# Turning k and q by the identity: one product over 128 rows, or two over 64 rows each

## The chip, the cores and the metric

The kernel runs on one core of a Trainium2 chip. The metric is the device time of one execution in microseconds (us); lower is better. Several runs of the kernel are timed, and one execution is recorded by the hardware profiler, which gives the rows that are quoted below.

## The reference, cut to what matters

The first half is a decaying linear attention over 4 batches, 8 heads, 768 positions and 64 channels, in blocks of 64 positions; the second is a mixer with a token part and a channel part.

```python
for b in range(nb):                       # blocks of 64 positions
    intra = einsum('bhic,bhjc->bhij', qb, kb) * Dmask
    intra = einsum('bhij,bhjd->bhid', intra, vb)
    inter = einsum('bhid,bhde->bhie', qb * lam_pow, kv_state)
    out[:, :, sl] = intra + inter
    kv_state = lam_block * kv_state + einsum('bhsd,bhse->bhde', kb * rev_pow, vb)
...
h = relu(x.T @ w_tok1) @ w_tok2
u = x + h.T
return u + relu(u @ w_ch1) @ w_ch2
```

The scores contract over the channels c. q and k arrive from memory with the positions on the partitions, and a product on TensorE contracts over the partitions, so both have to be turned first until the channels lie on the partitions.

## The kernel before

The attention runs over 16 items, each a batch and a pair of heads. For one item the kernel loads k as `kn` and q as `qn`, 128 positions on the partitions. It joins two 64-position blocks to chunks of 128 positions, six chunks a head.

**What is turned, and how.** `turn_k` turns k of every item: 6 products of a 128x128 block with the identity, three into one PSUM bank (h = 0, a bank of the rotating group "sh"), three into another (h = 1, bank "xT"). After each three, ScalarE copies the bank (128x384) to one contiguous half of `kT` (L233). `turn_q_rows` does the same for q (L245, L246), for the first 8 items only (NQ = 8); later items turn q on VectorE (L238). Within a half, the two 64-partition row groups of `kT` and `qT` hold the two 64-position groups or heads that `scores` later contracts apart.

**Who reads the result.** `scores` (L320) multiplies rows 0 to 63 and 64 to 127 of `kT` and `qT` as separate products, alternating between two PSUM banks; its first half (h = 0) reads columns 0 to 383, its second half columns 384 to 767. `scale_q` (L268, GpSimd) reads `qT` too.

**The order around it.** Every engine's queue keeps the order in which the program issues its instructions. Iteration i of the main loop issues on TensorE: `scores(i+1)` (L320), `carry(i)` (L348), `outputs(i, 0)` (L361), `state(i+1)` (the kv products, L281), `outputs(i, 1)` (L361), the turns of item i+2, and then for i of at least 0 two `turn_back` (xp, L386) with the products of the mixer's token part (ph L499, pu L520) placed around them from i = 4 on. On ScalarE the copies of the turns stand behind the copy of `outputs(i, 1)` (L368) and in front of the scaling of k (L262), the conversions of weights (L415, L416, L429) and the casts of `turn_back` (L392). Iterations -2 and -1 have no `turn_back`: there the scores of the item follow its turns at once.

```python
    for i in range(-2, NI):
        if 0 <= i + 1 < NI:
            scores(i + 1)
...
        if i + 2 < NI:
            turn_k(i + 2, 0)
            turn_k(i + 2, 1)
            if i + 2 < NQ:
                turn_q_rows(i + 2, 0)
                turn_q_rows(i + 2, 1)
```

The bank "xT" is used by `carry` for half of its output, by `turn_k` for h = 1 and by `turn_q_rows` for h = 1, one after the other; each must wait until the last reader has copied the bank out.

Of the kernel before, what the change touches and what calls it, by code (L numbers as in the profile page):

```python
# [9 lines left out]
F32 = mybir.dt.float32  # L10
# [15 lines left out]
def kernel(  # L26
# [23 lines left out]
    nc = tc.nc  # L50
    B, H, S, D = q.shape
# [3 lines left out]
    P = 128  # L55
# [36 lines left out]
    def all_of(nm, n):  # L92
        while not all((nm, i) in ready for i in range(n)):
            waiting.popleft()()
# [5 lines left out]
    ident = upool.tile([P, P], F32, name="ident")  # L100
# [10 lines left out]
    def bank(tag, nm, n):  # L111
        nonlocal shared
        if tag == "sh":
            tag = f"sh{shared % 3}"
            shared += 1
        return ps.tile([P, n], F32, tag=tag, bufs=4 if tag == "sc" else 1, name=nm)
# [6 lines left out]
    ap = att.enter_context(tc.tile_pool(name="att", bufs=1))  # L123
# [9 lines left out]
    loaded = {}  # L133
# [67 lines left out]
    def rows_of(x):  # L201
        return slice(x * D, (x + 1) * D)
# [5 lines left out]
    n = 1  # L208
    while n < P:
        nc.vector.tensor_mul(  # L210
            out=lams[:, :, n : 2 * n], in0=lams[:, :, 0:n], in1=lams[:, :, n - 1 : n].broadcast_to([P, 2 * NP, n])
# [3 lines left out]
    for h in range(2):  # L215
        r = rows_of(h)
# [4 lines left out]

    kTs, qTs, qss, kds, weights_of, scored = {}, {}, {}, {}, {}, {}

    def turn_k(i, h):
        kn, _ = loaded[i]
        if h == 0:
            kTs[i] = ap.tile([P, S], F32, tag="kT", bufs=2, name=f"kT{i}")
        kt = bank("xT" if h else "sh", f"kt{i}{h}", 3 * P)
        for m in range(3):
            nc.tensor.transpose(  # L230
                out=kt[:, m * P : (m + 1) * P], in_=kn[:, h, m].rearrange("p x d -> p (x d)"), identity=ident
            )
        nc.scalar.copy(out=kTs[i][:, 3 * h * P : (3 * h + 3) * P], in_=kt)  # L233

    def turn_q(i):
        qTs[i] = ap.tile([P, S], F32, tag="qT", bufs=2, name=f"qT{i}")
        if i >= NQ:
            nc.vector.transpose(out=qTs[i], in_=loaded[i][1])  # L238

    def turn_q_rows(i, h):  # L240
        qt = bank("xT" if h else "sh", f"qt{i}{h}", 3 * P)
        hs = slice(3 * h * P, (3 * h + 3) * P)
        for m in range(3):
            ms = slice((3 * h + m) * P, (3 * h + m + 1) * P)
            nc.tensor.transpose(out=qt[:, m * P : (m + 1) * P], in_=loaded[i][1][:, ms], identity=ident)  # L245
        nc.scalar.copy(out=qTs[i][:, hs], in_=qt)  # L246

    def scale_k(i):
        b, p = pairs[i]
# [14 lines left out]
    def scale_q(i):  # L264
        b, p = pairs[i]
        qss[i] = ap.tile([P, 2, 3, P], F32, tag="qs", bufs=2, name=f"qs{i}")
        for h in range(2):
            nc.gpsimd.tensor_mul(  # L268
                out=qss[i][:, h],
                in0=qTs[i].rearrange("p (h m i) -> p h m i", h=2, i=P)[:, h],  # L270
                in1=lamp[:, p, h, None, :].broadcast_to([P, 3, P]),
            )
# [40 lines left out]
    def scores(i):  # L313
        for h in range(2):
            scored[i, h] = sc = [bank("sc", f"sc{i}{x}{h}", 3 * P) for x in range(2)]
            for m in range(3):
                ms = slice((3 * h + m) * P, (3 * h + m + 1) * P)
                for x in range(2):
                    r = rows_of(x)
                    nc.tensor.matmul(  # L320
                        out=sc[x][:, m * P : (m + 1) * P],
                        lhsT=kTs[i][r, ms],
                        rhs=qTs[i][r, ms],
                        start=True,
                        stop=True,
                    )

    def weigh(i, h):
        b, p = pairs[i]
        for x in range(2):  # L330
            weights_of[i, x, h] = a = ap.tile([P, 3, P], F32, tag="a", bufs=8, name=f"a{i}{x}{h}")
            nc.vector.tensor_mul(  # L332
                out=a,
                in0=scored[i, h][x].rearrange("p (c i) -> p c i", i=P),
                in1=mask[:, 2 * p + h, None, :].broadcast_to([P, 3, P]),
            )
# [274 lines left out]
    def block(k, t):  # L611

        (b, c), (b1, c1) = divmod(2 * k, 3), divmod(2 * k + 1, 3)
        i, j = 3 * (b * NP + t) + c, 3 * (b1 * NP + t) + c1
        return U[:, i : j + 1 : j - i]
# [55 lines left out]
    for i in range(-2, NI):  # L671
        if i == 0:
            nc.vector.memset(scr[:, 3072:], 0)
        if i == NP:
            all_of("w1", 3)
        spare = 30 if i == 6 else 7
        if 0 <= i + 1 < NI:
            scores(i + 1)
            scale_q(i + 1)
            weigh(i + 1, 0)  # L680
        if i >= 0:
            carry(i)
            outputs(i, 0)
        place = state(i + 1) if 0 <= i + 1 < NI else None
        if 0 <= i + 1 < NI:
            weigh(i + 1, 1)
        if i >= 0:
            outputs(i, 1)
        if i + 2 < NI:
            turn_q(i + 2)  # L690
        work = [groups.popleft() for _ in range(take.get(i, 0))]
        if i + 2 < NI:
            if 0 < i + 2 < NP:
                masks(i + 2)
            turn_k(i + 2, 0)
            turn_k(i + 2, 1)
            if i + 2 < NQ:
                turn_q_rows(i + 2, 0)
                turn_q_rows(i + 2, 1)
        if place:  # L700
            place()
        if 1 <= i < NP:
            scale_k(i + 2)
        busy = i >= 8 and len(work) == 5
        if not busy:
            later(*((1 + (i < 6), 1, True) if i >= 4 else (4 if i > 1 else 1, 3)))
        n = early.get(i, len(work) // 4)
        cuts = [0, n, max(n, (3 * len(work) + 1) // 4 if len(work) > 2 else len(work) // 2), len(work)]
        for n in range(3):
            for f in work[cuts[n] : cuts[n + 1]]:  # L710
                f()
                if n == 2 or not busy:
                    later(2 if f in hidden else 1)
            if n < 2 and i >= 0:
                turn_back(i, n)
            if n == 0 and i + 2 < NI and not 1 <= i < NP:
                scale_k(i + 2)
            if n < 2 and i >= 0 and (n == 1 or not busy):
                later(*((1 + (i < 6), 1, n == 1) if i >= 4 else (3, 2) if (i, n) == (3, 1) else (2, 1, True)))
        if 1 <= i < 4:  # L720
            load_w2(i - 1)
        if 0 <= i + 3 < NI and i >= -1:
            load_v(i + 3)
        if -1 <= i < 2:
            load_w1(2 * i + 2, 2 * i + 4)
        if i + 4 < NI:
            load_kq(i + 4)
        if i in loads:
            x = loads.index(i)
            while read < x - 1:  # L730
                later(1)
            load_piece(x // 2, x % 2, words(3)[:, :2048] if x % 2 else scr[:, :2048])
        if 0 <= i < 3:
            convert_w1(i)
        if 2 <= i < 4:
            convert_w2(i - 2)
        if i == 3:
            convert_w2(2)
        if i == 11:
            later(99)  # L740
        if i in turns:
            x = turns.index(i)
            ng, piece = divmod(x, 2)
            a, sg = (words(3) if x % 2 else scr)[:, 2048:3072], scr[:, 3072:]
            waiting.extend(convert_piece(words(3)[:, :2048] if x % 2 else scr[:, :2048], a, sg))
            waiting.append(was_read)
            if ng > 0:
                waiting.append(lambda ng=ng, piece=piece, a=a: park(ng, piece, a))
            elif piece == 0:
                waiting.extend([lambda: None] * 2)  # L750
                waiting.extend(combine(0, lambda: wa, a))
            else:
                waiting.append(lambda a=a: park(0, 1, a))
                waiting.extend([lambda: None] * 2)
                waiting.extend(split_c2(0, lambda: wa, a))
        if i == 13:
            waiting.extend(raw_operand(0, 1, oa, nc.gpsimd, nc.gpsimd))
        if i == 13:
            waiting.extend(raw_operand(0, 2, oa, nc.gpsimd, nc.gpsimd))
# [58 lines left out]
    hs, c_of = {}, {}  # L818
# [524 lines left out]
    for n in range(NQD):  # L1343
        r, g = divmod(n, NG)
        for s in range(7):
# [69 lines left out]
            else:  # L1415
                if n == NG and s == 0:
                    tasks.extend(lambda q_=q_: mm2(NG - 1, 1 - q_ // 4, q_ % 4) for q_ in range(8))
                if n == NG and s == 1:
                    for i in range(4):
                        x = tp.tile([P, 2, CB], F32R, tag="tt", bufs=4, name=f"tt{i}")  # L1420
                        tiles.extend((x[:, 0], x[:, 1]))
                if n == NG + 1 and s == 1:
# [7 lines left out]
                    for t in ("c2h", "c2l"):  # L1430
                        x = w2b.tile([P, JG, DM], F32R, tag=t, name=f"{t}x")
# [31 lines left out]
        if n == NG - 1:  # L1463
# [8 lines left out]
            for t in ("c2h", "c2l"):  # L1472
                x = wa.tile([P, JG, DM], F32R, tag=t, name=f"{t}x")
# [45 lines left out]
```

## Time and profile before

| what | value |
|---|---|
| median of 3 runs | 554.84 us (554.48 to 555.19) |
| span of the profiled execution, first to last instruction | 552.4 us |
| left of the median outside that span | 2.4 us |
| TensorE busy | 537.1 us, 97% of the span |
| TensorE weight loads busy | 455.1 us, 82% |
| VectorE busy | 386.8 us, 70% |
| ScalarE busy | 250.2 us, 45% |
| GpSimd busy | 275.9 us, 50% |

For the profiled execution the span is what is recorded; the runs that were timed give the total beside it. Busy time of TensorE counts a product from its start to its modelled end. Products are pipelined, so neighbouring ones overlap in these records, and the distance from one start to the next is what a product costs in a stream.

### The profile page before, as it was taken

Reading aid. Unit: us, or ns where it says so; the run is one execution under the profiler, and the core shown is the slowest. Engines: PE = TensorE matmul, PEld = TensorE weight load, DVE = VectorE, ACT = ScalarE, POOL = GpSimd, SP = SyncE. Lnnn points to the kernel's source line nnn. Section 1 sums busy time; section 2 is a strip of 40 time slices with the busy share of each in tenths; the row PEclk is TensorE's granted clock in tenths of the full one; section 3 lists DMA queues with packets and bytes.
Section 4 is the critical chain, followed back from the end, with each engine's and each line's share of the span. In section 5 each row is a group of like instructions: output and inputs, shape, how many; then the busy total and the mean of one; then the engine's idle time right before and its main releaser. Section 6 shows DMA issues by size and latency. Waiting matters only on the chain.

```text
span 552.4 us, 9745 instructions
## 1 busy us (share of the span) xinstructions
PE 537.1 (97%) x3710; PEld 455.1 (82%) x3710; DVE 386.8 (70%) x588; ACT 250.2 (45%) x463; POOL 275.9 (50%) x264
## 2 busy tenths in 40 slices
PE   6999999999999999999999999999998999999996
PEld 5888989999999988788888888888886888888885
DVE  4667776677865868688995657498578864474464
ACT  3477544654534456455554344344464343233111
POOL 5555636552442777556769635545878123141000
PEclk9999999999999999999999999999999999999999
DMA  9999878698500497956777899677346987554007
GB/s 188 245 264 220 189 143 222 143 201 199 133 1 6 172 296 253 361 190 250 285 284 268 179 239 304 206 246 273 133 125 211 205 197 294 225 169 156 0 2 151
DMA packets 162942, 108.12 MB, mean 196 GB/s; under 512 B 132560, under 2 KB 147408, under 8 KB 162896
## 3 DMA queue, kind: packets, MB, share of 16 engines
q1 hardware_dynamic: 153168, 86.92, 58.4%
q10 hardware_dynamic: 9728, 20.58, 10.0%
q8 instruction: 29, 0.48, 0.4%
q14 instruction: 17, 0.14, 0.1%
HBM read 75.50 MB, written 31.98 MB: 195 GB/s over the span
## 4 chain that ended last, share of the span: by engine, by line
PE 81%; DVE 6%; ACT 5%; DMA 4%; POOL 2%; issue 2%; SPq 1%; DVEq 0%; ACTq 0%
PE b L858 15%; PE gb L1114 9%; PE po L1059 9%; PE d L858 7%; PE gc L1114 7%; PE ph L499 6%; PE pu L520 5%; PE sc L320 4%; PE xT L361 4%; PE a L858 4%; DMA raw<-in_moe_w_ch_dram 3%; PE xT L348 2%; PE gb L1059 2%; PE gc L1059 2%; PE kv L281 2%
## 5 line engine op out<-in xcount | busy, mean ns | idle before, releaser
L302 POOL COPY st<-sv 64x192 f32<-64x192 f32 (+1 forms) x32 | 15.7, 492 | 58.8 <-DVE sv L289 57.9
L1072 DVE TENSOR_TENSOR uT<-po,uT 128x512 f32<-128x512 f32 x48 | 32.8, 684 | 10.2 <-PE po L1059 9.6
L1059 PE MATMUL po<-hh,c2l 128*128 128x512 f32 x96 | 37.8, 394 | 0.0
L1059 PE MATMUL po<-hl,c2h 128*128 128x512 f32 x96 | 37.7, 392 | 0.0
L1059 PE MATMUL po<-hh,c2h 128*128 128x512 f32 x96 | 37.6, 392 | 0.0
L368 ACT COPY uT<-xT 128x384 f32<-128x384 f32 x32 | 15.2, 479 | 47.2 <-PE xT L361 47.2
L332 DVE TENSOR_TENSOR a<-sc,mask 128x384 f32<-128x384 f32 x64 | 32.1, 543 | 2.4 <-PE sc L320 2.3
L268 POOL TENSOR_TENSOR qs<-qT,lamp 128x384 f32<-128x384 f32 x32 | 32.6, 1040 | 0.0
L879 POOL TENSOR_TENSOR hl1x<-t,hh1x 128x512 fp32r<-128x512 f32 x8 | 10.6, 1326 | 41.8 <-ACT hh1x L873 41.8
L1129 DVE TENSOR_TENSOR uT<-gb,uT 128x512 f32<-128x512 f32 x40 | 26.1, 683 | 3.8 <-PE gb L1114 3.8
L393 DVE TENSOR_TENSOR xlo<-xp,xhi 128x384 fp32r<-128x384 f32 x32 | 17.7, 552 | 15.7 <-ACT xhi L392 15.2
L499 PE MATMUL ph<-xhi,w1h 128*128 128x256 f32 x96 | 28.3, 295 | 0.3 <-DVE hl L504 0.3
L499 PE MATMUL ph<-xhi,w1l 128*128 128x256 f32 x96 | 27.2, 283 | 0.0
L499 PE MATMUL ph<-xlo,w1h 128*128 128x256 f32 x96 | 27.1, 283 | 0.0
L361 PE MATMUL xT<-a,vn 128*64 128x128 f32 x384 | 27.1, 277 | 0.0
L320 PE MATMUL sc<-qT,kT 64*128 64x128 f32 x384 | 27.1, 290 | 0.0
L320 PEld LDWEIGHTS sc<-qT,kT 64*128 64x128 f32 x384 | 23.9, 197 | 3.0 <-issue 1.2
L858 PE MATMUL b<-o,c1h 128*128 128x512 f32 x72 | 25.2, 391 | 0.0
L858 PE MATMUL a<-o,c1h 128*128 128x512 f32 x72 | 25.2, 391 | 0.0
L879 POOL TENSOR_TENSOR tt<-t,tt 128x512 fp32r<-128x512 f32 x12 | 17.0, 1420 | 14.6 <-ACT tt L873 14.6
L520 PE MATMUL pu<-w2h,hh 128*128 128x384 f32 x64 | 23.2, 363 | 0.9 <-DVE uT L525 0.5
L289 DVE TENSOR_TENSOR_SCAN sv<-keep,kv 128x320 f32<-128x320 f32 x16 | 13.1, 816 | 13.3 <-PE kv L281 6.6
(417 smaller groups left out, 1737.6 us busy)
## 6 DMA issues: line engine op xcount, KB each, us to landing
c1h<-k SPq DMA_DIRECT2D x12, 896.0 KB, 5.5
c1l<-k SPq DMA_DIRECT2D x12, 896.0 KB, 7.6
raw<-in_moe_w_ch_dram SPq DMA_DIRECT2D x7, 1024.0 KB, 5.7
vn<-in_v_dram SPq DMA_DIRECT2D x16, 384.0 KB, 6.1
k<-c1h ACTq DMA_DIRECT2D x6, 896.0 KB, 5.2
k<-c1l ACTq DMA_DIRECT2D x6, 896.0 KB, 4.1
out_dram<-y SPq DMA_DIRECT2D x72, 64.0 KB, 2.5
c2lx<-k SPq DMA_DIRECT2D x7, 512.0 KB, 4.2
```

Of the source, the lines that this page charges most:

```text
L268: nc.gpsimd.tensor_mul(out=qss[i][:, h], in0=qTs[i].rearrange("p (h m i) -> p h m i", h=2, i=P)[:, h], in1=lamp[:, p, h, None, :].broadcas ...
L320: nc.tensor.matmul(out=sc[x][:, m * P : (m + 1) * P], lhsT=kTs[i][r, ms], rhs=qTs[i][r, ms], start=True, stop=True,)
L332: nc.vector.tensor_mul(out=a, in0=scored[i, h][x].rearrange("p (c i) -> p c i", i=P), in1=mask[:, 2 * p + h, None, :].broadcast_to([P, 3, P]),
L361: nc.tensor.matmul(out=xT[h * D : (h + 1) * D, m * P : (m + 1) * P], lhsT=vns[i][:, h, c, :], rhs=weights_of[i, x, h][:, m, :], start=Fals ...
L499: nc.tensor.matmul(out=ph, lhsT=w[:, c, fs], rhs=x[:, c], start=(i == 0), stop=(i == 3 * NC - 1))
L520: nc.tensor.matmul(out=pu, lhsT=h[:, kk, cs], rhs=w[:, kk, ss], start=(i == 0), stop=(i == 3 * NK - 1))
L858: nc.tensor.matmul(out=c[into], lhsT=w[:, WI[o], ct], rhs=x[:, ct], start=(first and i == 0), stop=(i == 5), skip_group_check=True,)
L879: nc.gpsimd.tensor_sub(out=B_[key][1], in0=src, in1=B_[key][0].bitcast(F32))
L1059: nc.tensor.matmul(out=po, lhsT=w[:, jj, cs], rhs=h, start=(i == 0), stop=(i == 3 * JG - 1), skip_group_check=n >= NG)
L1072: nc.vector.tensor_add(out=ub, in0=two(po), in1=ub)
L1114: nc.tensor.matmul(out=G[into, t], lhsT=w2[:, v, j, t * P : (t + 1) * P], rhs=x, start=(o in (5, 1, 2) and not second and i == 0), stop=(i ...
L1129: nc.vector.tensor_add(out=ub, in0=two(G[into, t]), in1=ub)
```

## The change

Each block of 128 rows is turned by two products of 64 rows: rows 0 to 63 with the upper left 64x64 of the identity into the "sh" bank, rows 64 to 127 with the lower right 64x64 into the "xT" bank. The six blocks of an item are issued in turn, the two halves of a block one after the other, and all twelve products come before the two copies. Each bank now holds one 64-row half of all six blocks, and each copy writes every other run of 64 columns of `kT` or `qT`.

```diff
-    def turn_k(i, h):
+    def turn(i, to, block, nm):
+        banks = [bank("xT" if y else "sh", f"{nm}{i}{y}", 3 * P) for y in range(2)]
+        for n in range(6):
+            for y in range(2):
+                r = rows_of(y)
+                nc.tensor.transpose(out=banks[y][:, n * D : (n + 1) * D], in_=block(n)[r], identity=ident[r, r])
+        view = to.rearrange("p (n y s) -> p n y s", y=2, s=D)
+        for y in range(2):
+            nc.scalar.copy(out=view[:, :, y], in_=banks[y].rearrange("p (n s) -> p n s", s=D))
+
+    def turn_k(i):
         kn, _ = loaded[i]
-        if h == 0:
-            kTs[i] = ap.tile([P, S], F32, tag="kT", bufs=2, name=f"kT{i}")
-        kt = bank("xT" if h else "sh", f"kt{i}{h}", 3 * P)
-        for m in range(3):
-            nc.tensor.transpose(
-                out=kt[:, m * P : (m + 1) * P], in_=kn[:, h, m].rearrange("p x d -> p (x d)"), identity=ident
-            )
-        nc.scalar.copy(out=kTs[i][:, 3 * h * P : (3 * h + 3) * P], in_=kt)
+        kTs[i] = ap.tile([P, S], F32, tag="kT", bufs=2, name=f"kT{i}")
+        turn(i, kTs[i], lambda n: kn[:, n // 3, n % 3].rearrange("p x d -> p (x d)"), "kt")
...
-    def turn_q_rows(i, h):
-        qt = bank("xT" if h else "sh", f"qt{i}{h}", 3 * P)
-        hs = slice(3 * h * P, (3 * h + 3) * P)
-        for m in range(3):
-            ms = slice((3 * h + m) * P, (3 * h + m + 1) * P)
-            nc.tensor.transpose(out=qt[:, m * P : (m + 1) * P], in_=loaded[i][1][:, ms], identity=ident)
-        nc.scalar.copy(out=qTs[i][:, hs], in_=qt)
+    def turn_q_rows(i):
+        turn(i, qTs[i], lambda n: loaded[i][1][:, n * P : (n + 1) * P], "qt")
...
-            turn_k(i + 2, 0)
-            turn_k(i + 2, 1)
+            turn_k(i + 2)
             if i + 2 < NQ:
-                turn_q_rows(i + 2, 0)
-                turn_q_rows(i + 2, 1)
+                turn_q_rows(i + 2)
```

## Rows read from the trace of the kernel before

**Rows 1.** The page: engines, busy us, share of the span, instructions; then the chain by engine
```profile
PE 537.1 (97%) x3710; PEld 455.1 (82%) x3710; DVE 386.8 (70%) x588; ACT 250.2 (45%) x463; POOL 275.9 (50%) x264
...
PE 81%; DVE 6%; ACT 5%; DMA 4%; POOL 2%; issue 2%; SPq 1%; DVEq 0%; ACTq 0%
```

**Rows 2.** The chain that ended last, first items: start us, us, what
```profile
7.01 0.88 PE qt L245 x3
7.88 2.86 PE sc L320 x24
...
13.22 0.55 PE qt L245 x3
```

**Rows 3.** The same chain from 18.2 us, iteration 0
```profile
18.30 0.49 ACT uT L368
...
18.82 0.87 ACT kT L233 x2
```

**Rows 4.** Tile kt: duration ns min/median/max, first and last start, forms
```profile
L230 PEld LDWEIGHTS kt<-ident,kn x96: 137/140/232, 4.3 to 150.0; 128*128 128x128 f32 x96
L230 PE MATMUL kt<-ident,kn x96: 272/273/477, 4.3 to 150.1; 128*128 128x128 f32 x96
L233 ACT COPY kT<-kt x32: 478/484/500, 5.2 to 150.4; 128x384 f32<-128x384 f32 x32
```

**Rows 5.** Tile sc, products of 64 rows
```profile
L320 PEld LDWEIGHTS sc<-qT,kT x384: 182/188/336, 7.8 to 157.5; 64*128 64x128 f32 x192
L320 PE MATMUL sc<-qT,kT x384: 271/272/577, 7.8 to 157.6; 64*128 64x128 f32 x192
```

**Rows 6.** Tile kv, products with 64 moving columns
```profile
L281 PE MATMUL kv<-vn,kd x320: 218/222/367, 10.7 to 159.9; 128*64 128x64 f32 x160
```

**Rows 7.** TensorE in order of time, iteration 0: start us, us, what, [idle before]
```profile
18.18 0.87 PE L230 MATMUL kt<-ident,kn 128*128 128x128 f32 x6
18.89 0.49 PE L245 MATMUL qt<-ident,qn 128*128 128x128 f32 x3
19.74 0.55 PE L245 MATMUL qt<-ident,qn 128*128 128x128 f32 x3 [0.36 <-ACT kT L233]
20.12 0.82 PE L386 MATMUL xp<-ident,uT 128*128 128x128 f32 x6
20.87 1.61 PE L320 MATMUL sc<-qT,kT 64*128 64x128 f32 x24
...
24.01 0.75 PE L281 MATMUL kv<-vn,kd 128*64 128x64 f32 x20
```

**Rows 8.** ScalarE in order of time, iteration 0
```profile
18.82 0.86 ACT L233 COPY kT<-kt 128x384 f32<-128x384 f32 x2
19.57 0.50 ACT L246 COPY qT<-qt 128x384 f32<-128x384 f32 x1
20.32 0.48 ACT L246 COPY qT<-qt 128x384 f32<-128x384 f32 x1 [0.25 <-PE qt L245]
```

**Rows 9.** TensorE in order of time, iteration -1
```profile
11.73 0.87 PE L230 MATMUL kt<-ident,kn 128*128 128x128 f32 x6
...
13.70 1.61 PE L320 MATMUL sc<-qT,kT 64*128 64x128 f32 x24
```

**Rows 10.** TensorE in order of time, iteration -2
```profile
4.31 1.71 PE L230 MATMUL kt<-ident,kn 128*128 128x128 f32 x6 [4.31 <-DMA kn<-in_k_dram]
```

**Rows 11.** TensorE in order of time, iteration 7, an item without q turns
```profile
83.81 0.88 PE L230 MATMUL kt<-ident,kn 128*128 128x128 f32 x6
84.46 0.44 PE L520 MATMUL pu<-w2h,hh 128*128 128x384 f32 x1
84.74 0.34 PE L520 MATMUL pu<-w2h,hl 128*128 128x384 f32 x1
84.92 0.34 PE L520 MATMUL pu<-w2l,hh 128*128 128x384 f32 x1
```

**Rows 12.** The chain in iteration 3
```profile
42.14 0.56 ACT kd L262
```

## The prediction

> **What bounds the kernel now.** I read the page's busy shares first, then the chain of waits by engine: TensorE is busy for 97% of the span and carries 81% of the chain [rows 1]. A busy TensorE is not yet a TensorE that does useful work all the time, so next I followed the chain in order of time through the attention, where all the turns lie. In the first iterations it does not stay on TensorE. In iteration 0 it goes from the copy of the outputs to the two copies of kT, all on ScalarE [rows 3], and back to TensorE with the second three turns of q. The reader should see there that TensorE stands idle for 0.36 us until ScalarE has copied kT [rows 7]: the "xT" bank has one copy, and q's second half needs it. The third thing to read is TensorE and ScalarE in order of time, to see which work runs beside which [rows 7, 8]: q's first three turns run while ScalarE still copies kT, and the first copy of qT is out before the second three turns are done. The fourth is the later items without turns of q [rows 11], where the next products follow the turns without a wait.
>
> **What a whole turn costs.** In the stream of six xp turns the step from start to start is (0.82 - 0.273) / 5 = 0.109 us [rows 4, 7]. The six of kt take 0.87 us, 0.05 more than xp, which is the first step after a change of the array's form (the products before them have 64 columns).
>
> **What a half turn costs.** No row shows a turn over 64 rows; two other products bracket it. The score products use row halves with 128 moving columns and come every (1.61 - 0.272) / 23 = 0.058 us [rows 5, 7], about half of 0.109: the two row halves do work side by side. The kv products have 64 moving columns and come every (0.75 - 0.222) / 19 = 0.028 us, so two in 0.056 [rows 6, 7]. A pair of half turns has both: row halves, and 64 moving columns. The lower end for a pair is half of a whole turn, 0.054 us; the upper end is a pair of score products, 0.116 us, where the 64x128 weight load and not the moving columns sets the step. The weight loads tell which is nearer: a score load of 64x128 takes 188 ns, that of a whole turn 140 ns with twice the rows [rows 4, 5]. Turns are thus loaded faster than ordinary products, for a reason that lies in the turn and not in its rows. I take 0.058 us a pair.
>
> The Trainium skill, in "TensorE: Matmul & The Clock Gate", section "LDWEIGHTS (loading the stationary operand)", says that a load costs its columns divided by 1.2, whatever its rows. By that rule each half would load for an estimated 107 ns, more than its 64 columns take to move, and splitting would save nothing per block; the 140 ns of a turn against the 188 ns of a score load speak against using one figure for both, and by the rule the sum is that of the second rival below.
>
> **A change of form.** The qt products end at 19.74 + 0.55 = 20.29 and xp, of the same form, starts at 20.12, 0.17 before that end. The xp end at 20.94 and the score products, of 64 rows, start at 20.87, only 0.07 before [rows 7]. So a change of form costs 0.10, and another 0.05 in the first step. The new turns add one such change to every item: from 64 rows back to 128.
>
> **Twelve half turns.** First to last pair 5 x 0.058 + 0.05 = 0.34 us; with the 0.22 that a product of 64 columns lasts [rows 6] they end 0.56 after they start, where six whole turns took 0.87. The next product of another form comes at 0.56 - 0.07 = 0.49, with the slower first step 0.54; before it came at 0.87 - 0.17 = 0.70. A turn saves 0.16, half of what its shorter products promise. For pu the same comes out: its second product stood 0.93 after the first kt (84.74 - 83.81), with a first step of 0.28 against 0.18 [rows 11], and will stand at 0.49 + 0.28 = 0.77.
>
> **Items 8 to 15, only k.** Eight turns at 0.16: -1.3 us. Their copies are not on the way of the next products. This holds where TensorE sets the pace; where VectorE does, it is less, so 0 to 1.3.
>
> **Items 2 to 4.** kt starts at 18.18 and ends at 18.74. ScalarE copies the outputs until 18.79 [rows 3] and starts on kT at 18.82 as before; shorter turns gain nothing there. Both copies are done at 19.68, and q's turns, which now all need "xT" from their second product on, start at 19.74. Before, only three were left at this point, and half of q was about to be copied [rows 8]. Now twelve halves run to 20.30, and both copies come after: 20.33 to 21.19, with 0.86 for the two as for kT [rows 8]. The scores read both interleaved halves at once, so they start 0.06 later at 21.25, where they started at 20.87 [rows 7]. The xp products lie between (20.23 to 21.10) and no longer cover the copies. +0.38 us in each of three items: +1.1. Behind the late copies stand the scaling of k and the casts on ScalarE, and scale_q on GpSimd; they move by the same 0.4 and are taken in by it.
>
> **Item 1.** No xp stands between turn and scores, and before, the scores began on the half that was there. kt runs 11.73 to 12.29, copies 12.32 to 13.18, q's turns 13.24 (13.22 before [rows 2]) to 13.80, copies 13.83 to 14.69, scores 14.75 against 13.70 [rows 9]: +1.05.
>
> **Item 0.** Here all runs at about half the pace (1.71 us for six turns [rows 10]). q's second half begins at 7.01 and its three turns take 0.88 [rows 2]; as pairs, at twice 0.058, some 0.3 less, to 7.57. Then two copies to 8.46 and the scores at 8.52, against 7.88 in the chain: about +0.7 with the 0.07 by which products start ahead of their piece in the chain.
>
> **Items 5 to 7.** In iteration 3 the chain runs through ScalarE: k's scaling stands behind qT's second copy [rows 12] and moves by the same 0.38; 0 if that copy is not what holds it. Items 6 and 7 are followed by products that don't need qT; there only the turns count: after the wait, xp or ph came 0.55 - 0.17 = 0.38 later, now 0.54. +0.16 each, 0.3 in all.
>
> **Sum.** 0.7 + 1.05 + 1.1 + 0.4 + 0.3 - 1.3 = +2.3 us. On the profiled execution's 552.4 us span that is 554.7; 2.4 us lie outside the span in the median of 554.84, so 557.1. The copies cost nothing new of themselves: 384 columns each as before, their runs cut to 64.
>
> **Rivals.** *The early loss is taken up (not slower).* Items 0 to 7 lose 3.6 us. If a later step of the attention is held by something that doesn't move with them, such as a transfer of weights or a conversion that VectorE and ScalarE have to finish anyway, the 3.6 vanish there and the 1.3 of the later items stay: 553.5. It decides from 1.3 us taken up upward (about 555.8 at that point). For it speaks that the chain leaves TensorE for 19% of the span [rows 1]; against it, that these steps stand in program order behind the copies that move, and that the DMA share of the chain is 4%. Chance 0.1.
>
> *The split saves nothing.* A pair takes 0.116, because the halves load at the score products' pace or don't overlap as turns. Then twelve halves end after 0.85, as six whole ones did, and the changed order of copies is all that is left: scores at 21.78 (+0.91) in items 2 to 5, +1.6 in item 1, about +1.0 in item 0, 0.7 in items 6 and 7, and in items 8 to 15 +0.13 each for the change of form: 3.6 + 1.6 + 1.0 + 1.4 + 1.0 = +8.7, 563.5. The page's rule above leads here. For it: only the 48 ns between two weight loads argue for a shorter load. Chance 0.2.
>
> *Halves one after the other, each at 0.111.* Some 0.58 more in each of 24 turns on top of that: about 577. The score products speak against it. Chance 0.03.
>
> The forecast has the remaining 0.67. Its own range is 556.4 (no loss in items 5 to 7) to 558.5, with 559 if the slow pace at the start lasts through item 1's scores, which took 2.86 us in the chain at that pace and 1.61 after it [rows 2, 9]. The range for 8 in 10 takes in the second rival and leaves out the first where it is complete: 554.6 to 564.2. A difference under 0.2%, 1.1 us, can't be told from no change here. Faster needs the first rival nearly whole: 0.06; within 0.2%, the rest of it and a small forecast: 0.11; slower 0.83.
>
> **What the profile after would show.** Pairs of half turns 0.058 apart, six in 0.56 with their end; kT's copies in iteration 0 where they were, relative to the copy of the outputs; no turn of q before them; TensorE idle for about 0.9 us instead of 0.36 there; the scores waiting for qT in items 1 to 4; in the later items the next product 0.16 sooner after kt. The forecast is wrong if the pairs are 0.11 apart, if the scores don't wait for both copies of qT, or if the shift at 62 us (about +3.6) is gone before 160 us by more than the 1.3 that the later items give back.

## The result, and the profile after

The changed kernel takes 560.72 us in the median of 4 runs (559.59 to 561.91), the kernel before 554.66: a ratio of 1.011, 95% interval 1.0098 to 1.0123. The way was forecast, the size was not: +6.1 us where +2.3 stood, though inside the range (554.6 to 564.2). The profiled execution took 560.19 us with a span of 558.4.

The page, which answers to [rows 1]: TensorE has 144 products more and is busy for 1.2 us less, in a span 6.0 us longer.

```profile
PE 535.9 (96%) x3854; PEld 453.1 (81%) x3854; DVE 388.0 (69%) x588; ACT 250.1 (45%) x463; POOL 275.7 (49%) x264
```

The tile kt, as in [rows 4]: duration min/median/max, first and last start, forms.

```profile
L229 PEld LDWEIGHTS kt<-ident,kn x192: 134/140/226, 4.8 to 156.3; 64*128 64x128 f32 x192
L229 PE MATMUL kt<-ident,kn x192: 221/223/367, 4.8 to 156.4; 64*128 64x64 f32 x192
L232 ACT COPY kT<-kt x32: 479/484/489, 6.2 to 157.0; 128x384 f32<-128x384 f32 x32
```

The weight load of a half turn is recorded with the 140 ns of a whole one, and a product lasts 223 ns, as the kv products with 64 columns did (222) [rows 6]. The copies cost what they cost before (484 ns), although they write runs of 64.

TensorE in order of time, from item 0's first turn to iteration 0 (compare [rows 10], [rows 9] and [rows 7]): start, us, what, idle time before and what ended it.

```profile
4.79 0.58 PE L229 MATMUL kt<-ident,kn 64*128 64x64 f32 x6 [4.79 <-DMA kn<-in_k_dram]
...
7.13 0.90 PE L229 MATMUL qt<-ident,qn 64*128 64x64 f32 x11 [0.27 <-ACT kT L232]
8.90 2.93 PE L319 MATMUL sc<-qT,kT 64*128 64x128 f32 x24 [0.88 <-ACT qT L232]
...
13.03 0.90 PE L229 MATMUL kt<-ident,kn 64*128 64x64 f32 x12
...
14.88 0.58 PE L229 MATMUL qt<-ident,qn 64*128 64x64 f32 x11 [0.89 <-ACT kT L232]
16.36 2.19 PE L319 MATMUL sc<-qT,kT 64*128 64x128 f32 x24 [0.90 <-ACT qT L232]
...
22.31 0.59 PE L229 MATMUL kt<-ident,kn 64*128 64x64 f32 x12
22.96 0.27 PE L229 MATMUL qt<-ident,qn 64*128 64x64 f32 x1
23.90 0.58 PE L229 MATMUL qt<-ident,qn 64*128 64x64 f32 x11 [0.67 <-ACT kT L232]
24.42 0.87 PE L385 MATMUL xp<-ident,uT 128*128 128x128 f32 x6
25.46 1.61 PE L319 MATMUL sc<-qT,kT 64*128 64x128 f32 x24 [0.17 <-ACT qT L232]
```

In iteration 0 the twelve halves of k end 0.59 us after their start (0.56 was forecast, 0.87 stood before). One half of q follows, into the free bank; the second needs the other bank, and eleven halves wait until k has been copied out. Then the scores wait for both copies of q: they start 3.15 us after the first turn of k, where it was 20.87 - 18.18 = 2.69 [rows 7].

ScalarE in the same iteration (compare [rows 8]):

```profile
22.43 0.48 ACT L367 COPY uT<-xT 128x384 f32<-128x384 f32 x1 [0.76 <-PE xT L360]
22.99 0.86 ACT L232 COPY kT<-kt 128x384 f32<-128x384 f32 x2
24.55 0.86 ACT L232 COPY qT<-qt 128x384 f32<-128x384 f32 x2 [0.70 <-PE qt L229]
```

Before, the first copy of q stood at 19.57, joined to k's two. Now ScalarE stands idle for 0.70 us until q's halves are done.

Where the 6.0 us of span arose, by the first start of kt in an item (from TensorE in order of time):

| stretch | before, us | after, us | forecast | measured |
|---|---|---|---|---|
| start to item 0's turn | 4.31 | 4.79 | 0 | +0.48 |
| turn of item 0 to turn of item 2 | 13.87 | 17.52 | +1.75 | +3.65 |
| item 2 to item 6 | 29.17 | 30.99 | +1.5 | +1.82 |
| item 6 to item 8 | 23.30 | 23.81 | +0.3 | +0.51 |
| item 8 to item 15 | 78.83 | 78.88 | -1.1 | +0.05 |
| item 15 to the end | 402.90 | 402.41 | -0.2 | -0.49 |

The loss in items 2 to 7 is near the forecast. The first row is the landing of the first k, before any turn; in the other runs it came 0.05 to 0.52 us later than in the trace before, also where items 0 and 1 were turned as before, so it is not put down to the change. Two entries are far from the forecast: the first two items lost 1.9 us more, and the later items gave nothing back. The first is seen in the stage's windows: us, then busy time of TensorE, weight loads, VectorE, ScalarE and GpSimd (with the number of instructions), then the granted clock, the DMA share and GB/s. Three windows of the kernel after, and one of the kernel before:

```profile
11.00:14.00 3.00, 2.98 (x41) 2.50 (x39) 1.39 (x4) 0.04 (x1) 1.19 (x2) 1.00 1.34 218
14.00:18.00 4.00, 2.22 (x33) 2.09 (x35) 3.34 (x8) 1.69 (x4) 3.26 (x6) 0.90 1.31 220
18.00:19.50 1.50, 1.50 (x24) 1.28 (x24) 0.35 (x1) 0.00 (x0) 0.99 (x2) 0.50 1.14 287
```

```profile
14.00:18.00 4.00, 4.00 (x88) 3.76 (x85) 2.54 (x6) 0.77 (x2) 3.32 (x4) 1.00 1.30 213
```

From 14 to 18 us TensorE is busy for 2.22 of 4.00 us, waiting twice for 0.9; then its granted clock is 0.50, the lower level of 1.2 GHz, while it ends the scores of item 1 and starts on the outputs of item 0. In the kernel before it is busy all through 14 to 18 us, and the clock shows 1.00 in every one of these windows. The 1.00 of the first window is no measure of the pace: twelve halves take 0.90 us at 13.03 us and 0.59 later, so TensorE is still slow there, where the kernel before had six turns in 0.87 us at 11.73 us [rows 9].

The second entry is seen in the later items. The waits of TensorE's weight loads (PEld) for ScalarE's copy of the outputs (uT) from 70 to 170 us: who waited for whom, us in total, times, longest.

```profile
PEld pu L519 <- ACT uT L367: 0.8, 4, 0.2
PEld xp L385 <- ACT uT L367: 0.4, 2, 0.2
PEld ph L498 <- ACT uT L367: 0.4, 2, 0.2
```

Eight items, eight waits of 0.2 us, none of which stood in the trace before. The product after k's turn takes the shared bank from which ScalarE copies half of the outputs (L367). That copy ends about 0.6 us after the first turn of k, whichever way k is turned, and the next product starts 0.65 us after that turn in both kernels (before, 0.71 in two of the eight items). Before, the six whole turns lasted as long as the copy; ScalarE in the kernel before, in the iteration of [rows 11]:

```profile
83.93 0.48 ACT L368 COPY uT<-xT 128x384 f32<-128x384 f32 x1 [0.76 <-PE xT L361]
```

### The profile page after: what moved, and what is told of

The parts are those of the page before. It is cut to its first block, busy times and chain, and to the rows that moved or that the text cites. A ratio compares the mean times of both kernels' runs of the same rounds, so it can differ in the third digit from the quotient of the medians.

```text
span 558.4 us, 10027 instructions
## 1 busy us (share of the span) xinstructions
PE 535.9 (96%) x3854; PEld 453.1 (81%) x3854; DVE 388.0 (69%) x588; ACT 250.1 (45%) x463; POOL 275.7 (49%) x264
## 4 chain that ended last, share of the span: by engine, by line
PE 65%; DVE 5%; DMA 4%; ACT 2%; issue 1%; DVEq 0%; ACTq 0%
PE b L855 15%; PE gb L1111 9%; PE po L1056 8%; PE d L855 7%; PE gc L1111 7%; DMA raw<-in_moe_w_ch_dram 4%; PE pu L519 4%; PE a L855 4%; PE ph L498 3%; PE gb L1056 2%; PE gc L1056 2%; PE xT L360 1%; PE sc L319 1%; PE xT L347 1%; PE xp L385 1%
## 5 line engine op out<-in xcount | busy, mean ns | idle before, releaser
L367 ACT COPY uT<-xT 128x384 f32<-128x384 f32 x32 | 15.3, 480 | 49.2 <-PE xT L360 49.2
L319 PE MATMUL sc<-qT,kT 64*128 64x128 f32 x384 | 27.6, 294 | 2.3 <-ACT qT L232 2.1
L319 PEld LDWEIGHTS sc<-qT,kT 64*128 64x128 f32 x384 | 24.4, 199 | 5.3 <-ACT qT L232 3.5
```

Source lines behind the costliest of these rows:

```text
L319: nc.tensor.matmul(out=sc[x][:, m * P : (m + 1) * P], lhsT=kTs[i][r, ms], rhs=qTs[i][r, ms], start=True, stop=True,)
```

## The experiments

Each ratio is to the kernel before, timed beside it on the same chip. Two theories stood after the result. The first: the order of turns and copies costs some 0.46 us in each early item, the clock 1.6 to 1.9 us at the start, and a bank takes the later items' gain. The second: 64-row products cost time themselves, in every item alike.

**Which items lose.** `whole_for_two` turns items 0 and 1 as before, and the rest by halves; `halves_for_two` is its counterpart.

```diff
-            turn_k(i + 2)
+            if i + 2 >= 2:        # whole_for_two;  i + 2 < 2 in halves_for_two
+                turn_k(i + 2)
+            else:
+                whole_k(i + 2, 0)
+                whole_k(i + 2, 1)
...                                # q in the same way
```

> Items 0 and 1 are turned as before (whole products, a copy after each three), items 2 to 15 by halves. The theory: of the 6.0 us of span that the change costs, 3.7 us arise before item 2's turn starts, because the scores of items 0 and 1 follow the turns directly and because TensorE's clock then rises about 2.4 us later and falls back once (granted 0.50 in 18.0 to 19.5 us). With whole turns there the 3.7 us are gone: +2.3 us over the kernel before, about 557.0. The rival, that every item with turns of q loses the same: two of eight such items are spared, a quarter of 6, so +4.5 us, about 559.2.

Measured: 557.75 us, ratio 1.0051 (1.0038 to 1.0065). The start took 13.63 us from turn to turn against 13.87 before, so its loss is gone. Items 2 to 5 lost 0.43 to 0.46 each. What the theory did not have is one more fall of the clock: item 6 lost 1.76 us, where it loses 0.30 in the changed kernel. TensorE was busy for 2.48 of the 4.00 us from 48 to 52, where the kernel before has 3.78:

```profile
48.00:52.00 4.00, 2.48 (x44) 1.97 (x40) 3.97 (x9) 2.62 (x6) 2.52 (x3) 0.92 1.29 245
52.00:54.00 2.00, 2.00 (x12) 1.88 (x10) 1.97 (x3) 1.45 (x3) 1.88 (x3) 0.50 1.12 203
```

> Only items 0 and 1 are turned by halves, k and q; items 2 to 15 as before. The counterpart of whole_for_two, which left +3.0 us without them. The theory, that these two items carry the copies' delay (1.7 us as forecast) and most of the late clock: +3 to +3.7 us, about 558, and the clock falls back before 21 us as in the changed kernel; nothing is lost or gained after item 2. The rival, equal loss per item: +1.5 us, about 556.2.

Measured: 557.53 us beside 553.82, ratio 1.0066 (1.0052 to 1.0079). The start took 16.57 us, +2.7, and no item after it lost anything (the shift is 3.03 us at item 2 and 2.97 at item 15). The recorded execution took 556.54 us, 1.0 us under the median. The clock fell here too (granted 0.51 in this window):

```profile
15.00:18.50 3.50, 3.11 (x28) 2.89 (x32) 2.03 (x4) 0.34 (x1) 3.31 (x4) 0.51 1.25 218
```

Equal loss per item is refuted by both: items 0 and 1 alone cost 3.0 us in the trace and 3.7 in the median, items 2 to 15 alone 3.0 in the median, about 1.5 of it by the fall of the clock in item 6.

**The clock.** `after_filled` gives TensorE products to do in its waits; their results are overwritten.

```diff
+        for n in range((8 if i < 2 else 10) if nm == "qt" else 0):
+            r = rows_of(0)
+            nc.tensor.transpose(out=banks[0][:, n % 6 * D : (n % 6 + 1) * D], in_=block(n % 6)[r], identity=ident[r, r])
...
+            for _ in range(4 if i < 2 and h == 0 else 0):
+                nc.tensor.transpose(out=sc[0][:, :P], in_=ident, identity=ident)
```

> The changed kernel with extra products whose results are overwritten, put where TensorE stands idle: before q's twelve halves the upper halves once more (10 products of 64 rows, 0.56 us, in a wait of 0.67 to 0.89 us), and ahead of the scores of items 0 and 1 four turns of the identity (0.85 us at the slow pace, in a wait of 0.88 and 0.90 us). The theory, that 1.9 of the 6.0 us are TensorE's clock, which rises later and falls back (0.50 in 18.0 to 19.5 us) because TensorE does less at the start: the clock rises near 11.4 us as before and stays, and the time falls by 1.5 to 2 us to about 558.9, though TensorE does more. The rival, that the late start comes from waits alone: no gain, 560.7 or slower.

Measured: 559.22 us, ratio 1.0086 (1.0073 to 1.0099). With more work the kernel is 1.5 us faster. The start took 15.90 us in place of 17.52, and the clock stayed up:

```profile
14.00:18.00 4.00, 3.30 (x55) 2.74 (x57) 3.65 (x8) 1.41 (x4) 3.22 (x5) 1.00 1.31 220
18.00:21.00 3.00, 3.00 (x74) 2.71 (x66) 0.99 (x3) 0.81 (x2) 1.03 (x2) 1.00 0.67 201
```

TensorE in order of time at the start of `after_filled` (its four turns of the identity, L319, write to sc):

```profile
4.66 0.58 PE L232 MATMUL kt<-ident,kn 64*128 64x64 f32 x6 [4.66 <-DMA kn<-in_k_dram]
...
9.67 2.73 PE L324 MATMUL sc<-qT,kT 64*128 64x128 f32 x24
12.33 0.80 PE L283 MATMUL kv<-vn,kd 128*64 128x64 f32 x20
13.07 0.59 PE L232 MATMUL kt<-ident,kn 64*128 64x64 f32 x12
...
16.09 1.61 PE L324 MATMUL sc<-qT,kT 64*128 64x128 f32 x24 [0.31 <-ACT qT L235]
...
20.56 0.59 PE L232 MATMUL kt<-ident,kn 64*128 64x64 f32 x12
```

The scores of item 0 stand here in the kernel before:

```profile
7.81 2.94 PE L320 MATMUL sc<-qT,kT 64*128 64x128 f32 x24
```

| stretch of the start, us | before | after | `after_filled` |
|---|---|---|---|
| item 0's first turn to its scores | 3.50 | 4.11 | 5.01 |
| those scores to item 1's first turn | 3.92 | 4.13 | 3.40 |
| item 1's first turn to its scores | 1.97 | 3.33 | 3.02 |
| those scores to item 2's first turn | 4.48 | 5.95 | 4.47 |

With the clock up, item 1 loses 1.05 us between its turns and its scores, and nothing behind them. The 1.6 us that come back are a net figure: the added products hold item 0's scores back by 0.9 us. By stretches the changed kernel's 3.65 us are some 2.0 of the clock (0.21 and 1.47 behind the scores, and 1.36 - 1.05 = 0.31 in item 1's turns) and some 1.7 of the copies (0.61 + 1.05), an estimate from these three traces; the forecast had 1.75 for the copies. `before_warm` asks whether the clock at the start is worth something to the kernel before.

```diff
+    warm = bank("sc", "warm", P)
+    for _ in range(13):
+        nc.tensor.transpose(out=warm, in_=ident, identity=ident)
```

> The kernel before with 13 turns of the identity, written to a bank that nothing reads, between the end of the identity's making (1.4 us) and the landing of the first k (4.3 us), where TensorE stands idle. The theory of the clock: with work from 1.4 us on, the half pace of the first items ends some 3 us sooner than at 11.4 us, and half of that is gained: 553.2 (-1.5 us). The rival, that the pace of the start is bound to something other than TensorE's own work: 554.7, no difference.

Measured: 553.92 us, ratio 0.9988 (0.9980 to 0.9997). The full pace is there earlier, the scores of item 0 take 1.61 us and not 2.94, but little is gained. TensorE in order of time (the view begins at 3 us, with the last seven of the thirteen), and the piece of the chain that ends before item 1's q:

```profile
2.72 1.70 PE L189 MATMUL warm<-ident 128*128 128x128 f32 x7
...
7.60 1.61 PE L323 MATMUL sc<-qT,kT 64*128 64x128 f32 x24
```

```profile
6.09 6.29 DMA qn<-in_q_dram
```

Item 1's q lands at 12.38 us, and that sets the start then. The theory was right on the pace and wrong on its worth: in the kernel before, the slow first items lie in front of that transfer, and q's turns of item 1 begin at 12.44 us there and at 12.43 here. In the changed kernel the slow pace reaches past it, to the turns at 13.03 us. This is the one version faster than both, by 0.7 us (0.2 to 1.1).

**The later items.** `halves_from_eight` splits only k of items 8 to 15; `k8_other_bank` adds one line after it, `shared += 1`, by which the next product takes the following shared bank.

> Only k of items 8 to 15 is turned by halves; all else is as before. The prediction on record gave these eight turns -1.3 us (0.16 each), about 553.4. The theory after the result: the product that follows takes the shared bank that held half of the outputs, and it waits for ScalarE's copy of them, which ends as late as before; so no difference, 0 to +0.2 us, about 554.8.

Measured: 554.7 us, ratio 0.9998 (0.9989 to 1.0007): no difference, and eight waits of 0.2 us for the copy of the outputs as in the changed kernel.

> As halves_from_eight, but after k's twelve halves one shared bank is passed over, so that the next product goes to the bank of the kv products, which VectorE has read by then, and not to the one that ScalarE still copies out. The theory, that this bank is what takes the gain away: the next product starts about 0.13 to 0.15 us sooner in up to eight items, -0.8 to -1.1 us, about 553.8. The rival, that the change of the array's form takes the gain: as halves_from_eight, 554.7.

Measured: 557.07 us, ratio 1.0048 (1.0036 to 1.0060). TensorE in iteration 8, in `halves_from_eight` and then in `k8_other_bank`:

```profile
95.97 0.59 PE L229 MATMUL kt<-ident,kn 64*128 64x64 f32 x12
96.61 0.39 PE L517 MATMUL ph<-xhi,w1h 128*128 128x256 f32 x1
```

```profile
95.09 0.59 PE L229 MATMUL kt<-ident,kn 64*128 64x64 f32 x12
95.61 0.39 PE L517 MATMUL ph<-xhi,w1h 128*128 128x256 f32 x1
```

The next product comes 0.52 us after the turn's start in place of 0.64. From item 9's turn to item 10's and from there to item 11's the time is 0.13 and 0.12 us shorter than before, about what was forecast for a turn (0.16). Item 8's next product came as early, but a later wait for VectorE took the gain. In iteration 9 the wait that takes the first one's place shows: the bank of the kv products is still being read by VectorE.

```profile
108.08 0.39 PE L517 MATMUL ph<-xhi,w1h 128*128 128x256 f32 x1 [1.70 <-DVE sv L307]
```

After that wait the clock falls once more (granted 0.60 from 108 to 112 us), and this one item is 2.9 us longer. The three intervals that follow are 0.13 to 0.21 us longer each: item 12 waits for VectorE again, and in items 13 and 14 a later product takes the bank of k's own turns and waits 0.3 us for ScalarE to copy them out.

```profile
PEld ph L517 <- ACT kT L232: 0.7, 2, 0.3
```

So the bank is shown to be what held the next product back, and the next bank in the round is worse for the kernel.

**Order against halves.** `whole_alternating` has the changed order with whole products.

```diff
         for n in range(6):
-            for y in range(2):
-                r = rows_of(y)
-                nc.tensor.transpose(out=banks[y][:, n * D : (n + 1) * D], in_=block(n)[r], identity=ident[r, r])
+            nc.tensor.transpose(out=banks[n % 2][:, n // 2 * P : (n // 2 + 1) * P], in_=block(n), identity=ident)
...
```

> Whole 128-row products in all items, but with the changed order: block by block into the two banks in turn, both copies after the last product, each copy taking every other block of 128 columns. The theory, that the loss comes from copies and turns that wait for each other and not from 64-row products: slower than the changed kernel, since six whole turns end 0.87 us after their start and not 0.56, twice per item with q; items 2 to 5 at about +0.95 each, items 0 and 1 at +3 to +5 with the late clock, items 6 and 7 at +0.5 each: 562 to 564. The rival, that half-row products or their change of the array's form are what costs: near the kernel before, 554.5 to 555.5.

Measured: 560.26 us, ratio 1.0097 (1.0083 to 1.0110), between the two and much nearer to the theory: the order alone costs what the change costs. Items 2 to 5 lost 0.54 to 0.77 us each, more than with halves (0.44 to 0.46) and less than expected; items 2 to 7 together lost 3.46 us, with halves 2.33. At the start 2.4 us were lost and not 3 to 5, with halves 3.65: TensorE was busier, 2.81 of the 4.00 us from 14 to 18, and the clock stayed at 1.00.

```profile
14.00:18.00 4.00, 2.81 (x39) 2.30 (x42) 3.09 (x7) 1.61 (x4) 3.42 (x6) 1.00 1.31 212
```

What halves save in items 2 to 7, whole turns save at the start.

`q_halves_from_two` and `k_halves_from_two` take the two tensors apart; items 0 and 1 are as before.

> Only q of items 2 to 7 is turned by halves; k and items 0 and 1 as before. The theory, that q's twelve halves all wait for k's copies and both copies of q come after them: the whole loss of whole_for_two, +0.46 us in items 2 to 5, +0.3 and +0.2 in items 6 and 7, +2.3 us, about 557; more, up to 558.6, if TensorE's clock falls back once as it did there. The rival, that k's and q's halves share the loss: half of it, 555.8.

Measured: 556.1 us beside 553.82, ratio 1.0038 (1.0026 to 1.0051). Items 2 to 5 lost 0.40 to 0.41 us each, nearly the 0.46 of the theory; item 6 lost nothing and item 7 0.17, where 0.3 and 0.2 stood. Without k's halves the clock did not fall.

> Only k of items 2 to 15 is turned by halves; items 0 and 1 and all of q as before. The theory, that ScalarE's copy of the outputs and not the turn of k sets the start of k's copies, and that q's order is what costs: no difference, 554.6, with iterations 0 to 2 at 7.16 us each as before. The rival, that the halves of k cost by their later first copy or their change of form: +0.3 to +0.46 in each of items 2 to 5, 556 or more.

Measured: 557.13 us beside 553.82, ratio 1.0058 (1.0045 to 1.0071), against the theory and far above it. Yet the attention is not where it is lost: items 2 to 5 took 0.04 us more each, and the last turn of k comes at the same time after the first. One transfer of weights near 216 us took 10.01 us (8.14 before), and the span ended 6.15 us after the start of the last product (5.11 before). `k_halves_again` is the same kernel on another chip.

> The kernel of k_halves_from_two once more, on whatever chip it gets. There the attention part took as long as before (last turn of k 0.1 us off), and 2.5 us were lost after it, in one transfer of weights of 10.01 us where 8.14 stood before and in the tail after the last product. If that belongs to the kernel, the time is again 3 us over the kernel before; if it belongs to that run's chip or placement, 554.5 to 555 beside a kernel before at 554.7, which is what the theory said of k's halves (no difference).

Measured: 557.53 us beside 554.49, ratio 1.0061 (1.0045 to 1.0077), with 10.22 us for the same transfer and 6.06 at the end:

```profile
216.34 10.22 DMA raw<-in_moe_w_ch_dram
```

It belongs to this kernel then, and not to the chip, and lies in transfers 60 us behind the turns. Why it does is open. `q_past_the_bank`, below, has some of it (9.08 us for the transfer, and 0.85 us more after item 15's turn); in the other runs that transfer takes 7.9 to 8.5 us. The changed kernel does not have it (its part after item 15's turn is 0.5 us shorter than before), so it is no part of the 6 us.

**The bank in q's way.** `q_past_the_bank` is the changed kernel with q's second bank from the shared group; `q_past_whole` the kernel before with the same.

```diff
-        banks = [bank("xT" if y else "sh", f"{nm}{i}{y}", 3 * P) for y in range(2)]
+        banks = [bank("xT" if y and nm == "kt" else "sh", f"{nm}{i}{y}", 3 * P) for y in range(2)]
```

> The changed kernel with one edit: q's lower halves go to a second shared bank and not to the bank that k's lower halves still hold, so q's turns need not wait for ScalarE to copy k. The theory: in items 2 to 5 the four copies then run without a gap and the scores start some 0.8 us sooner than in the changed kernel, 0.3 to 0.4 sooner than before; items 6 and 7 gain 0.5 each on the kernel before; item 1 keeps +0.4 and item 0 +0.7 with some of the late clock. Sum -1.3 to +1 us on the kernel before, about 555. The rival, that the wait for the bank is only covered time and the two copies after q's turns set the start of the scores anyway: as the changed kernel, 560.7.

Measured: 558.65 us, ratio 1.0076 (1.0063 to 1.0089), neither. The recorded execution took 560.26 us, 1.6 us over the median, so its trace shows more loss than the median has. Its start was 2.6 us longer than before, with a fall of the clock as in the changed kernel. Items 2 and 3 took 6.93 us each, 0.23 less than before; the theory had 0.3 to 0.4. From iteration 2 on VectorE is behind, and the new bank is held by its scan of kv:

```profile
45.26 0.58 PE L229 MATMUL qt<-ident,qn 64*128 64x64 f32 x11 [1.43 <-DVE sv L288]
```

```profile
46.00:50.00 4.00, 3.91 (x34) 3.22 (x32) 1.52 (x4) 4.00 (x9) 2.10 (x3) 0.57 1.06 266
```

After that wait the granted clock is 0.57 in the next 4 us, and item 5 alone is 2.3 us longer than before.

> The kernel before with one edit: the second half of q's whole turns goes to a shared bank in place of the one that k's second half holds. The theory, that the wait for k's copy holds the first eight items: about 0.3 us less per item in items 2 to 5 and 0.4 in items 6 and 7, 553 (-1.5 us), where VectorE has read the kv bank in time. The rival, that the wait for the kv bank takes its place, as in q_past_the_bank (0.85 and 1.43 us of waiting for it in iterations 2 and 3): 554.7 or slower.

Measured: 555.12 us, ratio 1.0012 (1.0003 to 1.0020). The rival: 0.28 us less in items 2 and 3, 0.3 and 0.9 more in items 4 and 5.

## Why the forecast was right and where it was wrong

The sum had +2.3 us, and the span grew by 6.0. Two terms make 3.1 of the 3.7 us between: items 0 and 1 (+1.75, measured +3.65) and the later items (-1.1 up to item 15's turn, measured +0.05). The rest is small: the first landing (+0.5), items 2 to 7 (+0.5), the part after item 15's turn (-0.3).

**What a half turn costs: right in size, its reason open.** Twelve take 0.59 us where 0.56 stood; (0.59 - 0.223 - 0.05) / 5 gives 0.063 us a pair, 0.058 was taken. The weight load of a half is 140 ns, that of a whole turn, so it was the turn and not the rows that made the load short, as the forecast said. That the load sets the step, on which the choice of 0.058 leaned, is not shown: two loads of 140 ns stand in every 0.063 us, so they overlap, and the moving columns fit as well (a whole turn and a pair of score products, with 128, come 0.109 and 0.116 us apart, a pair of halves, with 64, 0.063). The Trainium skill's rule on loads ("TensorE: Matmul & The Clock Gate", section "LDWEIGHTS (loading the stationary operand)"), columns divided by 1.2 whatever the rows, agrees in the rows, with 140 ns for 64 and for 128 of them [rows 4]. Its time for 128 columns, an estimated 107 ns, is neither the 140 ns of turns nor the 188 ns of score products [rows 4, 5], and the pairs are not that far apart; the measurement decides.

**Items 2 to 5: right in mechanism, 0.3 us short in all.** q's turns wait for k's copies, q's copies come after them, the scores wait for both. 0.46 per item was measured in items 2 to 4 where 0.38 stood, 0.44 in item 5. The experiment with q alone shows that q's order makes nearly all of it. "TensorEngine Tiling (Array Packing)" of the Trainium skill, section "Performance Considerations", warns that tiling speeds up TensorE and not the copies out of PSUM; these rows agree: four copies, 0.86 us for each two, set the pace of an early item, and turns that are faster but finish together feed them later.

**Items 8 to 15: wrong, 1.3 us.** The failed step is "Their copies are not on the way of the next products." The copies of the turns are not; the copy of the outputs is, one instruction ahead of them on ScalarE. Three shared banks go round, and the product after k's turn gets the one that this copy empties. Before, six whole turns covered the copy to within 0.05 us: in iteration 7 it ended at 83.93 + 0.48 = 84.41, and the next product began at 84.46 [rows 11], so no wait stood in the trace. The cover and the work were the same length, and shortening the cover gained nothing: the next product stayed at 0.65 us after the first turn, and came at 0.52 only in `k8_other_bank`, where 0.49 to 0.54 was forecast. A gain must name what the next instruction waits for, as a price of nothing must name its cover.

**Items 0 and 1: the term was 1.9 us too small.** The failed step is the clock: the sum reckons item 1 at full pace from 11.73 us on, as in the trace before, and all behind its scores at no loss. The copies' part was right in sum, +1.75 where some 1.7 were measured, in item 0 partly by luck: it counted three pairs of q from 7.01 us, where eleven halves were left, which took 0.90 us but began 0.4 us sooner after the first turn. The rest, some 2.0 us, is the clock. The forecast named the slow pace at the start, put 1.25 us on its lasting longer, and left it in the forecast's own range. What it lacked is that the change itself takes nearly half of TensorE's busy time out of just this stretch (2.22 of 4.00 us where 4.00 stood) and adds two waits of 0.9 us in item 1, and that the clock can fall back after it has risen. That it fell because of these waits is borne out by `after_filled`, where TensorE was given work in them; which of its waits matter was not taken apart.

**The rivals.** Nothing of the early loss was taken up later, against the first rival: the shift is 6.46 us at item 8 and 6.52 at item 15, with 0.48 of it from the first landing. The pairs were not 0.11 apart, against the second and third. The second rival's time (563.5) was nearer to the result than the forecast (2.8 us off, the forecast 3.6), for a wrong reason.

## What to carry to other kernels

Before pricing a shorter stretch on the busy engine as a gain, look at what its next instruction will wait for once it comes sooner: the bank it takes, and who copies that bank out. Two banks that are filled together are emptied together; where a copy per half used to start early, filling them in turn trades the engine's time for the copier's wait. And in a stage full of waits, work taken off TensorE can lower its clock, as in the start of this kernel, so the price of a wait there has two levels.

## What the runs showed of the hardware that was not expected

In the changed order, six whole turns and twelve half turns cost the kernel nearly the same time (560.26 and 560.72 us): the halves were 1.1 us ahead in items 2 to 7 and 1.2 behind at the start, where TensorE was busy for 2.22 of 4.00 us and the granted clock then went to 0.50; with whole ones it was busy for 2.81 and the clock stayed. The same fall followed a wait of 1.43 us in `q_past_the_bank` and one of 1.7 us in `k8_other_bank`. With thirteen turns of the identity ahead of it, and nothing else changed, TensorE was at its full pace before 7.6 us; up to then it had done nothing but turns. The clock column reads 1.00 from the start of every trace, also where six turns take 1.71 us in place of 0.87 [rows 7, 10]; for the first microseconds the pace has to be read from the products. Why one transfer of weights, 60 us behind the turns, took 2 us longer in both runs of one kernel is open.
